# Splits of pre-added weight blocks pinned behind the operation in front of them, and norm steps set further apart, in an attention, experts and squared-ReLU kernel

## The chip, the cores and the metric

The kernel runs on one core of a Trainium2 chip. The metric is the time of one execution on the device in microseconds (us); for each kernel it is measured several times and the median is taken. A profile is one further execution, taken with the hardware profiler: it has a span from the first to the last instruction, and a time of its own.

The core's engines work side by side: TensorE (PE in the profile, its weight loads PEld), VectorE (DVE), ScalarE (ACT), GpSimd (POOL) and SyncE (SP). Each runs its own instructions strictly in the order in which they stand, and an instruction that waits holds up those behind it on the same engine.

## What is computed

Three layers follow each other: windowed attention with a distance bias, a top-1 mixture of eight experts, and a dense layer with a squared ReLU. The change touches the last one alone. Cut to what matters:

```python
def _moe2_ref(x, w_in, w_out):
    h = x @ w_in
    r = np.maximum(h, 0.0)
    g = r * r
    return (g @ w_out).astype(np.float32)

# x: (2304, 512) from the experts, w_in: (512, 2048), w_out: (2048, 512), float32
```

## The kernel before

The last layer (`moe2`, L1366 on) works on the 2304 tokens in nine groups `G` of 256. Every float32 operand is split into two float16 numbers, a high and a low one, and a product is three float16 matmuls (high by high, high by low, low by high). Such a split is two instructions: ScalarE casts to the high half, DVE subtracts it for the low half.

For each group there is a norm (`norm`, L1102), a generator whose steps are run one by one with `next`:

- step 1: ScalarE takes the absolute values (`ab`, L1110), into the buffer `dec`
- step 2: PE sums them (L1115); DVE makes a power of two of the sums (`fac`, L1118 to L1120) and two diagonals `sd` from it (L1124)
- step 3: PE multiplies a matrix of ones by `sd` (L1129), which spreads the factor; DVE scales the group with it (L1130)
- step 4: four subtractions (L1137 to L1140) and the split into `hi` and `lo` (L1150, L1152)

The two halves `m` of the hidden dimension are then handled in turn. `wide1(G, m)` multiplies by `w_in` with seven products of 24 matmuls each (`product`, L1168) in the place of eight (Strassen-Winograd); their results are taken out of PSUM by ScalarE (`keep`, L1188) and DVE (`join`, L1189), squared and split (`square`, L1198; the split is L1195 and L1196). `wide2(G, m)` multiplies by `w_out` for the first three groups, the plain ones (`G < SG`, 3), with 48 matmuls (L1357 to L1359). From group 3 on, `seven` does this step with seven products too, and needs sums and differences of blocks of `w_out`: `T1` to `T4` of eight combined blocks.

The function `mix(k)` makes combined block `k`. Its first part is six additions and subtractions on GpSimd (L1272, L1276 to L1279), in a scratch that is a column of `yT` or `dec`; the first is made to wait for the last DVE instruction of the preceding `wide1` (`end_dve`). Its second part splits the four results: two casts on ScalarE (L1283) and two subtractions on DVE (L1284), queued behind `end_act` and `end_dve`. The table `MIXES` says at which point of the walk over the groups a block is touched: the first time a block is named its first part is issued, the second time its second part. The points are (G, 0) behind `wide2(G, 0)`, (G, 1) inside `wide1(G + 1, 0)` after its second pair of products, (G, 2) behind `wide2(G, 1)` or `seven`, and (G, 3) behind `wide1(G + 1, 1)`.

The norm of group `G + 2` is run inside the work on group `G`. `step` (L1396) issues its next step behind `end_act` and `end_dve`. In plain groups `wide2(G, 0)` calls it four times, once after each 12 matmuls.

Beyond such pins a scheduler orders each engine's queue. `issue_after` orders issue on the same engine and waits for nothing; `behind` is a true wait.

Of the kernel before, what the change touches and what calls it, by code (L numbers as in the profile page):

```python
# [43 lines left out]
RSC = 2.0 ** -9  # L44
# [3 lines left out]
GW = GT * P  # L48
SG = 3
SCRATCH = {0: 0, 1: 1, 2: 1, 3: 2, 4: 3}  # L50
MIXES = {(0, 0): (0,), (0, 1): (0, 1), (0, 2): (1, 2), (0, 3): (2, 3), (1, 0): (3, 4), (1, 2): (4, 5),
         (1, 3): (5,), (2, 0): (6,), (2, 2): (6, 7), (2, 3): (7,)}
STEPS = (((2, 6), ()), ((1, 5), (1,)), ((4,), (1,)), ((1, 5), (1,)), ((1, 5), (1,)), ((3,), (1, 3)), ((3,), (1, 3)),
         ((1, 3, 5, 7), (1, 3)))
SPARE = ((), (), (4, 5, 6, 7), (4, 5, 6, 7), (4, 5, 6, 7), (6, 7), (7,), ())
# [38 lines left out]
class K:  # L94
# [1007 lines left out]
    def norm(self, G, ab, tt):  # L1102


        nc, mp, V = self.nc, self.mp, self.nc.vector
        view = lambda o, n, dt: self.part(o, n, dt) if o is not None else             self.dec.bitcast(dt)[:, :n]
        ab = view(ab, 4 * GW, BF16).rearrange("p (c n) -> p c n", c=4)
        y = self.yT[:, :, G * GW:(G + 1) * GW]
        f = self.fac[G] = mp.tile([P, 2, GT], F32, tag="fac", bufs=4, name="fac")
        nc.scalar.activation(ab, y, AF.Abs)  # L1110
        yield
        l1 = self.bank([P, GT])
        for i in range(GT):
            for c in range(4):
                nc.tensor.matmul(l1[:, i:i + 1], ab[:, c, i * P:(i + 1) * P], self.onesb[:, 0:1],  # L1115
                                 start=c == 0, stop=c == 3)
        m, s = f[:, 0], f[:, 1]
        V.tensor_scalar(m, l1, TINY, HUGE, op0=ALU.max, op1=ALU.min)  # L1118
        V.tensor_single_scalar(m.bitcast(U32), m.bitcast(U32), 0x7F800000, op=ALU.bitwise_and)
        V.reciprocal(s, m)  # L1120
        sds = []
        for i in range(GT):
            sd = mp.tile([P, P], BF16, tag="sd", bufs=2, name="sd")
            V.tensor_scalar(sd, self.idf, s[:, i:i + 1], YSC, op0=ALU.mult, op1=ALU.mult)  # L1124
            sds.append(sd)
        yield
        sb = self.bank([P, GW])
        for i in range(GT):
            nc.tensor.matmul(sb[:, i * P:(i + 1) * P], self.onesb, sds[i], start=True, stop=True)  # L1129
        V.tensor_tensor(y, y, sb.unsqueeze(1).to_broadcast([P, 4, GW]), op=ALU.mult)  # L1130
        yield
        b = y.rearrange("p (h k) (t n) -> p h t k n", h=2, t=2)
        late = G >= SG + 2
        Q = nc.gpsimd if late else V
        t = view(tt, 4 * GW, F32)
        t1, t2, t3, t4 = (t[:, j * GW:(j + 1) * GW].rearrange("p (k n) -> p k n", k=2) for j in range(4))
        Q.tensor_tensor(t1, b[:, 0, 1], b[:, 0, 0], op=ALU.subtract)  # L1137
        Q.tensor_tensor(t2, b[:, 1, 1], t1, op=ALU.subtract)
        Q.tensor_tensor(t3, b[:, 1, 1], b[:, 0, 1], op=ALU.subtract)
        Q.tensor_tensor(t4, b[:, 1, 0], t2, op=ALU.subtract)  # L1140
        if late:
            yield
        hi, lo = self.xts[G] = [self.part(G % 2 * 7168 + 3584 * a, 14 * P, F16).rearrange("p (c n) -> p c n", c=14)
                                for a in range(2)]
        y = y.rearrange("p c (t n) -> p c t n", t=2)
        t = t.rearrange("p (c n) -> p c n", c=8)
        parts = ((0, y[:, :, 0]), (4, y[:, 2:, 1]), (6, t))
        for o, src in parts:
            n = src.shape[1]
            nc.scalar.copy(hi[:, o:o + n], src)  # L1150
            if not late:
                V.tensor_tensor(lo[:, o:o + n], src, hi[:, o:o + n], op=ALU.subtract)  # L1152
        yield
        for o, src in parts if late else ():
            n = src.shape[1]
            V.tensor_tensor(lo[:, o:o + n], src, hi[:, o:o + n], op=ALU.subtract)
        yield
# [22 lines left out]
    def wide1(self, G, m, between=lambda k: None):  # L1180


        nc, V = self.nc, self.nc.vector
        S1, S2, S3, S4, A11, A12, A22 = range(7)
        B11, B21, B22, T1, T2, T3, T4 = range(7)
        c = self.part(14336, 16 * P).rearrange("p (j i t n) -> p j i t n", j=4, i=2, t=2)
        u, p5, z, p1 = (self.part(22528 + 2048 * k, 4 * P).rearrange("p (j n) -> p j n", j=4) for k in range(4))
        keep = lambda dst, ps: nc.scalar.activation(dst, ps, AF.Copy, scale=RSC)  # L1188
        join = lambda dst, ps, x: V.scalar_tensor_tensor(dst, ps, RSC, x, op0=ALU.mult, op1=ALU.add)  # L1189
        mul = lambda *a: self.product(G, m, *a)  # L1190
        n = 2 if G < SG else 4
        g = self.gts[G, m] = [self.ring(F16, [P, 2, 8 * P]) for _ in range(n)]

        def halves(hi, lo, src):
            self.end_act = nc.scalar.copy(hi, src)  # L1195
            self.end_dve = V.tensor_tensor(lo, src, hi, op=ALU.subtract)  # L1196

        def square(i):  # L1198
            ci = c[:, :, i].rearrange("p j t n -> p j (t n)")
            if G < SG:  # L1200
                V.scalar_tensor_tensor(ci, ci, 0.0, ci, op0=ALU.max, op1=ALU.mult)  # L1201
                halves(*(t.rearrange("p i (j n) -> p i j n", j=4)[:, i] for t in g), ci)
                return
            nc.scalar.activation(ci, ci, AF.Relu)  # L1204
            nc.scalar.activation(ci, ci, AF.Square, scale=0.5)
            both = lambda t: (t[:, a].rearrange("p (o j n) -> p o j n", o=2, j=4) for a in range(2))
            if i == 0:
                V.tensor_tensor(p1, c[:, :, 0, 0], c[:, :, 0, 1], op=ALU.subtract)
                halves(*(t[:, 0] for t in both(g[3])), c[:, :, 0, 0])
                halves(*(t[:, 1] for t in both(g[3])), p1)  # L1210
                return
            V.tensor_tensor(p5, c[:, :, 0, 1], c[:, :, 1, 1], op=ALU.add)
            halves(*(g[0][:, a].rearrange("p (j n) -> p j n", j=4) for a in range(2)), ci)
            V.tensor_tensor(u, p5, c[:, :, 0, 0], op=ALU.subtract)
            halves(*both(g[1]), self.part(22528, 8 * P).rearrange("p (o j n) -> p o j n", o=2, j=4))
            V.tensor_tensor(z, c[:, :, 1, 0], u, op=ALU.subtract)
            halves(*(t[:, 0] for t in both(g[2])), z)

        keep(p1, mul(A11, B11))
        keep(u, mul(S2, T2))  # L1220
        V.tensor_tensor(u, u, p1, op=ALU.add)
        keep(p5, mul(S1, T1))
        V.tensor_tensor(z, u, p5, op=ALU.add)  # L1223
        between(0)
        join(c[:, :, 0, 0], mul(A12, B21), p1)
        join(c[:, :, 0, 1], mul(S4, B22), z)
        between(1)
        square(0)
        p7 = mul(S3, T3)
        join(c[:, :, 1, 1], p7, z)  # L1230
        join(u, p7, u)
        join(c[:, :, 1, 0], mul(A22, T4), u)
        square(1)
        between(2)
# [15 lines left out]
    def mix(self, k):  # L1250
# [19 lines left out]
        for o in range(2):  # L1270
            w = self.wo_s[8 * o + k]
            sum_ = Q.tensor_tensor(x[o], *(w[:, a].rearrange("p (o n) -> p o n", o=2) for a in range(2)), op=ALU.add)  # L1272
            if o == 0:
                self.behind(sum_, self.end_dve)
        t1, t3, t4, t2 = (x[o // 2][:, o % 2] for o in range(4))
        Q.tensor_tensor(t1, t3, t1, op=ALU.subtract)  # L1276
        Q.tensor_tensor(t3, t2, t3, op=ALU.subtract)
        Q.tensor_tensor(t2, t2, t1, op=ALU.subtract)
        Q.tensor_tensor(t4, t4, t2, op=ALU.subtract)  # L1279
        yield  # L1280
        with tc.issue_after(self.end_act.ins), tc.issue_after(self.end_dve.ins):
            for o in range(2):
                nc.scalar.copy(y[o][:, :, 0], x[o])  # L1283
                V.tensor_tensor(y[o][:, :, 1], x[o], y[o][:, :, 0], op=ALU.subtract)  # L1284
# [81 lines left out]
    def moe2(self):  # L1366
# [15 lines left out]
        def at(*key):  # L1382
            for n in MIXES.get(key, ()):
                if n in mixing:
                    for _ in mixing.pop(n):
                        pass
                else:
                    mixing[n] = self.mix(n)
                    next(mixing[n])

        mixing = {}
        for G in range(NG):
# [3 lines left out]
            def step():  # L1396
                with tc.issue_after(self.end_act.ins), tc.issue_after(self.end_dve.ins):
                    next(nr)

            if G < SG:  # L1400
                self.wide2(G, 0, lambda k: step())
            else:
                self.seven(G, 0, lambda k: step() if k == 5 else None)
            at(G, 0)
            if more:
                self.wide1(G + 1, 0, lambda k: step() if G >= SG and k < 2 else at(G, 1) if k == 1 else None)
            if G < SG:
                self.wide2(G, 1)
                if G + 1 == SG:
# [67 lines left out]
```

## Time and profile before

| | us |
|---|---|
| timed runs | 768.66, 773.87, 776.87 |
| their median | 773.87 |
| profiled execution, its own time | 769.61 |
| its span | 767.5 |
| PE busy in the span | 715.7 |
| DVE, ACT, POOL busy | 595.9, 444.2, 210.4 |

The span is divided about so: attention and experts until about 410, the plain groups 0 to 2 from there to about 545, then the groups with `seven`. Times in the rows are counted from the start of the span. A row of the timeline gives the start, the duration, engine, line, operation, what it writes and reads, how many instructions are merged in it, and in brackets how long the engine stood idle before it and what released it. A matmul's duration holds the way through the array, so the duration of one matmul is longer than the distance to the next.

### The profile page before, as it was taken

Reading aid. Unit: us, or ns where it says so; the run is one execution under the profiler, and the core shown is the slowest. Engines: PE = TensorE matmul, PEld = TensorE weight load, DVE = VectorE, ACT = ScalarE, POOL = GpSimd, SP = SyncE. Lnnn points to the kernel's source line nnn. Section 1 sums busy time; section 2 is a strip of 40 time slices with the busy share of each in tenths; the row PEclk is TensorE's granted clock in tenths of the full one; section 3 lists DMA queues with packets and bytes.
Section 4 is the critical chain, followed back from the end, with each engine's and each line's share of the span. In section 5 each row is a group of like instructions: output and inputs, shape, how many; then the busy total and the mean of one; then the engine's idle time right before and its main releaser. Section 6 shows DMA issues by size and latency. Waiting matters only on the chain. (4 is left out here: it accounts for less than half of the span.)

```text
span 767.5 us, 19611 instructions
## 1 busy us (share of the span) xinstructions
PE 715.7 (93%) x7979; PEld 603.0 (79%) x7979; DVE 595.9 (78%) x1454; ACT 444.2 (58%) x748; POOL 210.4 (27%) x247
## 2 busy tenths in 40 slices
PE   6989999998879899999898699999999999999996
PEld 5889899787645566788698377676799999999995
DVE  5898888854769988967898776977769696878672
ACT  5878898833456665664643333334657575757561
POOL 4583521434533110000000504733403021211011
PEclk9999999999989999999999989999999999999999
DMA  9895314776689676557614000000000000000000
GB/s 330 293 392 145 79 55 100 242 198 158 204 299 316 217 261 211 188 178 233 207 58 139 2 5 25 2 29 1 29 2 29 2 29 2 29 2 29 2 29 28
DMA packets 35656, 91.71 MB, mean 119 GB/s; under 512 B 5209, under 2 KB 13547, under 8 KB 35547
## 3 DMA queue, kind: packets, MB, share of 16 engines
q1 hardware_dynamic: 29803, 75.77, 30.5%
q0 software_dynamic: 5760, 14.65, 5.8%
q8 instruction: 64, 1.05, 0.6%
q14 instruction: 29, 0.24, 0.1%
HBM read 77.54 MB, written 13.04 MB: 118 GB/s over the span
## 5 line engine op out<-in xcount | busy, mean ns | idle before, releaser
L1176 PEld LDWEIGHTS <-wi 128*128 128x128 f16 x3024 | 172.7, 98 | 11.0 <-issue 9.3
L1309 PEld LDWEIGHTS <-wr 128*128 128x128 f16 x1008 | 98.1, 98 | 12.3 <-issue 1.0
L1195 ACT CAST wr<-work 128x1024 f16<-128x1024 f32 (+1 forms) x72 | 59.9, 832 | 59.2 <-DVE work L1201 42.4
L1176 PE MATMUL ps_a<-work,wi 128*128 128x128 f16 x1344 | 84.9, 220 | 0.0
L850 PE MATMUL ps_c<-work,wr 128*128 128x352 f16 (+5 forms) x256 | 75.1, 297 | 9.2 <-DVE work L799 8.2
L1176 PE MATMUL ps_b<-work,wi 128*128 128x128 f16 x1272 | 80.0, 220 | 1.4 <-DVEq L1064 1.4
L849 PE MATMUL ps_c<-work,wr 128*128 128x352 f16 (+5 forms) x256 | 75.0, 296 | 5.1 <-ACT yT L852 4.2
L851 PE MATMUL ps_c<-work,wr 128*128 128x352 f16 (+5 forms) x256 | 74.9, 296 | 0.0
L1196 DVE TENSOR_TENSOR wr<-work,wr 128x1024 f16<-128x1024 f32 (+1 forms) x72 | 68.9, 980 | 4.4 <-ACT wr L1195 4.4
L310 PE MATMUL ps_a<-yT,wr 128*128 128x192 f32 (+2 forms) x288 | 64.8, 346 | 6.4 <-DMA wr<-in_q_dram 4.7
L322 ACT ACTIVATE pb<-pb,nm 128x192 f32<-128x192 f32 (+2 forms) x144 | 56.3, 433 | 12.4 <-DVE nm L315 11.6
L1337 POOL DMA_INDIRECT out_dram<-o,oid x18 | 25.4, 1412 | 122.1 <-ACT o L1335 87.5
L770 DVE SCALAR_TENSOR_TENSOR wr<-rw,wr 128x1024 f16<-128x1024 f32 x40 | 48.7, 1219 | 8.9 <-ACT wr L769 8.7
L769 ACT ACTIVATE wr<-rw 128x1024 f16<-128x1024 f32 x40 | 42.1, 1058 | 23.1 <-DMA rw<-in_w_dram 22.2
L315 DVE CUSTOM_DVE_ANT_0 pb<-ps_a,bias 128x192 f32<-128x192 f32 (+2 forms) x144 | 44.1, 325 | 10.1 <-PE ps_a L310 9.4
L310 PEld LDWEIGHTS ps_a<-yT,wr 128*128 128x128 f32 x288 | 45.6, 201 | 7.7 <-DMA yT<-in_k_dram 6.4
L1272 POOL TENSOR_TENSOR yT<-wr 128x512 f32<-128x512 f16 x8 | 11.4, 1430 | 144.6 <-ACTq L1064 120.0
L1204 ACT ACTIVATE work<-work 128x1024 f32<-128x1024 f32 x24 | 25.4, 1058 | 38.3 <-DVE work L1189 38.3
L333 PE MATMUL ps_b<-cst,pb 128*128 128x128 f32 x256 | 44.0, 283 | 0.5 <-ACT pts L337 0.4
L851 PEld LDWEIGHTS <-wr 128*128 128x128 f16 x288 | 29.3, 102 | 19.1 <-issue 11.5
L850 PEld LDWEIGHTS <-wr 128*128 128x128 f16 x288 | 29.4, 102 | 14.5 <-issue 7.1
L778 POOL DMA_INDIRECT xg<-xd,idx x21 | 26.6, 1265 | 49.6 <-PE ps_d L786 42.4
(294 smaller groups left out, 1884.6 us busy)
## 6 DMA issues: line engine op xcount, KB each, us to landing
rw<-in_w_dram SPq DMA_DIRECT2D x40, 512.0 KB, 5.9
wi<-in_w_dram SPq DMA_DIRECT2D x20, 512.0 KB, 6.1
rw<-in_wo_dram SPq DMA_DIRECT2D x16, 512.0 KB, 4.2
rw<-in_wi_dram SPq DMA_DIRECT2D x32, 256.0 KB, 4.9
wr<-in_q_dram SPq DMA_DIRECT2D x14, 512.0 KB, 8.0
xd<-xhl POOLq DMA_DIRECT2D x16, 256.0 KB, 6.2
yT<-in_k_dram SPq DMA_DIRECT2D x7, 576.0 KB, 9.3
rw<-in_v_dram SPq DMA_DIRECT2D x12, 325.0 KB, 5.5
```

The costliest lines, as they stand in the source:

```text
L310: nc.tensor.matmul(ps[:, s, first:hi], q[g, u, hh // 4][:, hh % 4, s if u < 4 else 0, :], self.kt[g, hh // 2][:, hh % 2, key0:key0 + hi - ...
L315: self.last_ttr = nc.vector.tensor_tensor_reduce(out=pb[:, s, first:hi], in0=ps[:, s, first:hi], in1=self.bias[:, hh, first - lo:192], sca ...
L322: self.last_exp = nc.scalar.activation(pb[:, s, first:hi], pb[:, s, first:hi], AF.Exp, bias=nm[:, s:s + 1], scale=-1.0)
L333: nc.tensor.transpose(pt[:, t, :, s, :], pb[:, s, t * P:(t + 1) * P], self.idf)
L770: self.nc.vector.scalar_tensor_tensor(t[:, 1], st, sc, t[:, 0], op0=ALU.mult, op1=ALU.subtract)
L849: nc.tensor.matmul(py, wh, hh, start=fc == 0, stop=False)
L850: nc.tensor.matmul(py, wh, hl, start=False, stop=False)
L851: self.last_mm = nc.tensor.matmul(py, wl, hh, start=False, stop=fc == 7)
L1176: self.nc.tensor.matmul(ps[:, j], w[:, kp, a, w0 * P:(w0 + 1) * P], v[:, 2 * x + kp], start=kp + b == 0, stop=kp == 1 and b == 2)
L1195: self.end_act = nc.scalar.copy(hi, src)
L1196: self.end_dve = V.tensor_tensor(lo, src, hi, op=ALU.subtract)
L1309: nc.tensor.matmul(ps[n], x[:, v, j], y[j][:, w], start=m + i + j == 0, stop=m == 1 and i == 2 and j == 3)
```

## The change

Four things are edited. First, every operation that takes results out in `wide1` or ends a norm step (`keep`, `join`, `halves`, and the casts and subtractions at the end of `norm`) is remembered as `fin_act` or `fin_dve`, and `mix` queues its splits and its first addition behind these instead of `end_act` and `end_dve`. Second, block 4 is begun at (1, 1) and block 6 at (2, 1), inside `wide1`, not at (1, 0) and (2, 0). Third, in plain groups the call after the second 12 matmuls of `wide2(G, 0)` issues no norm step any more. Fourth, the step left over is issued in the next `wide1`, after its first three products.

```diff
@@ -48,8 +48,8 @@
-MIXES = {(0, 0): (0,), (0, 1): (0, 1), (0, 2): (1, 2), (0, 3): (2, 3), (1, 0): (3, 4), (1, 2): (4, 5),
-         (1, 3): (5,), (2, 0): (6,), (2, 2): (6, 7), (2, 3): (7,)}
+MIXES = {(0, 0): (0,), (0, 1): (0, 1), (0, 2): (1, 2), (0, 3): (2, 3), (1, 0): (3,), (1, 1): (4,), (1, 2): (4, 5),
+         (1, 3): (5,), (2, 1): (6,), (2, 2): (6, 7), (2, 3): (7,)}
@@ -1147,9 +1147,9 @@
         for o, src in parts:
             n = src.shape[1]
-            nc.scalar.copy(hi[:, o:o + n], src)
+            self.fin_act = nc.scalar.copy(hi[:, o:o + n], src)
             if not late:
-                V.tensor_tensor(lo[:, o:o + n], src, hi[:, o:o + n], op=ALU.subtract)
+                self.fin_dve = V.tensor_tensor(lo[:, o:o + n], src, hi[:, o:o + n], op=ALU.subtract)
@@ -1185,15 +1185,19 @@
-        keep = lambda dst, ps: nc.scalar.activation(dst, ps, AF.Copy, scale=RSC)
-        join = lambda dst, ps, x: V.scalar_tensor_tensor(dst, ps, RSC, x, op0=ALU.mult, op1=ALU.add)
...
+        def keep(dst, ps):
+            self.fin_act = nc.scalar.activation(dst, ps, AF.Copy, scale=RSC)
+
+        def join(dst, ps, x):
+            self.fin_dve = V.scalar_tensor_tensor(dst, ps, RSC, x, op0=ALU.mult, op1=ALU.add)
+
         def halves(hi, lo, src):
-            self.end_act = nc.scalar.copy(hi, src)
-            self.end_dve = V.tensor_tensor(lo, src, hi, op=ALU.subtract)
+            self.end_act = self.fin_act = nc.scalar.copy(hi, src)
+            self.end_dve = self.fin_dve = V.tensor_tensor(lo, src, hi, op=ALU.subtract)
@@ -1271,14 +1275,14 @@
             if o == 0:
-                self.behind(sum_, self.end_dve)
+                self.behind(sum_, self.fin_dve)
...
-        with tc.issue_after(self.end_act.ins), tc.issue_after(self.end_dve.ins):
+        with tc.issue_after(self.fin_act.ins), tc.issue_after(self.fin_dve.ins):
             for o in range(2):
                 nc.scalar.copy(y[o][:, :, 0], x[o])
                 V.tensor_tensor(y[o][:, :, 1], x[o], y[o][:, :, 0], op=ALU.subtract)
@@ -1398,12 +1402,12 @@
             if G < SG:
-                self.wide2(G, 0, lambda k: step())
+                self.wide2(G, 0, lambda k: step() if k != 1 else None)
...
-                self.wide1(G + 1, 0, lambda k: step() if G >= SG and k < 2 else at(G, 1) if k == 1 else None)
+                self.wide1(G + 1, 0, lambda k: step() if k == 0 or G >= SG and k == 1 else at(G, 1) if k == 1 else None)
```

In the changed file the lines from `join` on stand four to seven further down: the joins are L1196 instead of L1189, the squarings L1205 instead of L1201, the splits of a block L1288 instead of L1284, the matmuls of `wide2` L1361 to L1363 instead of L1357 to L1359.

On DVE, in plain group 0 behind `wide2(0, 0)`, the norm of group 2 and the splits of block 0 (the rows that write `xm`) stood so before:

```order
L1118 TENSOR_SCALAR fac<-ps_c 128x2
L1284 TENSOR_TENSOR xm<-yT,xm 128x2x256
L1119 TENSOR_SCALAR fac<-fac 128x2
L1284 TENSOR_TENSOR xm<-yT,xm 128x2x256
L1120 RECIPROCAL fac<-fac 128x2
L1124 TENSOR_SCALAR sd<-cst,fac 128x128 x2
L1165 SCALAR_TENSOR_TENSOR fac<-fac,og 128x2
```

and stand so in the change:

```order
L1118 TENSOR_SCALAR fac<-ps_c 128x2
L1119 TENSOR_SCALAR fac<-fac 128x2
L1120 RECIPROCAL fac<-fac 128x2
L1124 TENSOR_SCALAR sd<-cst,fac 128x128 x2
L1165 SCALAR_TENSOR_TENSOR fac<-fac,og 128x2
```

The two splits have left the norm's chain. Further on in the same queue of the change, inside `wide1(1, 0)`, they stand here (the joins are L1196, the squaring is L1205):

```order
L1196 SCALAR_TENSOR_TENSOR work<-ps_b,work 128x4x128
L1196 SCALAR_TENSOR_TENSOR work<-ps_c,work 128x4x128
L1288 TENSOR_TENSOR xm<-yT,xm 128x2x256 x2
L1205 SCALAR_TENSOR_TENSOR work<-work 128x4x256
L1196 SCALAR_TENSOR_TENSOR work<-ps_a,work 128x4x128
```

They moved behind the second join and in front of the first squaring. On PE, in the same place, the first matmul on `sd` stood behind 21 of the 24 matmuls of the first product of `wide1(1, 0)`; in the change it stands behind five, here with the last of the five and what follows:

```order
L1176 LDWEIGHTS wi_3339
L1176 MATMUL ps_b<-work,wi_3339 128x128
L1129 LDWEIGHTS onesb
L1129 MATMUL ps_a<-sd,onesb 128x128
L1176 LDWEIGHTS wi_3339
L1176 MATMUL ps_b<-work,wi_3339 128x128
L1176 LDWEIGHTS wi_3340
L1176 MATMUL ps_b<-work,wi_3340 128x128
L1129 LDWEIGHTS onesb
L1129 MATMUL ps_a<-sd,onesb 128x128
```

Two matmuls stand between the two on `sd`, as before. In group 1, PE had the pair on `sd` (into `ps_b`) in the middle of `wide2(1, 0)`, five matmuls behind the sums of L1115:

```order
L1357 LDWEIGHTS wr
L1357 MATMUL ps_d<-wr 128x512
L1129 LDWEIGHTS onesb
L1129 MATMUL ps_b<-sd,onesb 128x128
L1129 LDWEIGHTS onesb
L1129 MATMUL ps_b<-sd,onesb 128x128
L1358 LDWEIGHTS wr
```

and has it in the change at the end of `wide2(1, 0)`, in front of `wide1(2, 0)`:

```order
L1363 LDWEIGHTS wr
L1363 MATMUL ps_d<-wr 128x512
L1129 LDWEIGHTS onesb
L1129 MATMUL ps_b<-sd,onesb 128x128
L1129 LDWEIGHTS onesb
L1129 MATMUL ps_b<-sd,onesb 128x128
L1176 LDWEIGHTS wi_3339
```

The pair now has twelve matmuls between itself and the sums, which come one matmul later than before. Group 2 has the same two moves.

## Rows read from the trace of the kernel before

**Rows 1.** The page: each engine's busy us, share of the span, instructions.

```profile
PE 715.7 (93%) x7979; PEld 603.0 (79%) x7979; DVE 595.9 (78%) x1454; ACT 444.2 (58%) x748; POOL 210.4 (27%) x247
```

**Rows 2.** Waits of PE, 400 to 580 us: total us, times, longest.

```profile
PE ps_a L1129 <- DVE sd L1124: 6.5, 1, 6.5
...
PE ps_b L1129 <- DVE sd L1124: 1.4, 2, 0.9
PE ps_a L1115 <- ACT dec L1110: 0.8, 1, 0.8
PE ps_b L1115 <- ACT dec L1110: 0.7, 1, 0.7
PE ps_d L1309 <- DVE wr L1284: 0.6, 1, 0.6
```

**Rows 3.** Timeline of PE, 434 to 450 us: start, duration, instruction, idle before.

```profile
434.03 1.33 PE L1176 MATMUL ps_b<-work,wi 128*128 128x128 f16 x21
441.91 0.27 PE L1129 MATMUL ps_a<-sd,onesb 128*128 128x128 bf16 x1 [6.54 <-DVE sd L1124]
...
446.94 1.50 PE L1176 MATMUL ps_b<-work,wi 128*128 128x128 f16 x24
448.29 1.50 PE L1176 MATMUL ps_c<-work,wi 128*128 128x128 f16 x24
```

**Rows 4.** Timeline of DVE, 433 to 442 us.

```profile
433.10 1.15 DVE L1166 SCALAR_TENSOR_TENSOR fac<-fac 128x2 f32<-128x2 f32 x2
434.16 0.15 DVE L1118 TENSOR_SCALAR fac<-ps_c 128x2 f32<-128x2 f32 x1
437.32 1.23 DVE L1284 TENSOR_TENSOR xm<-yT,xm 128x512 f16<-128x512 f32 x1 [3.01 <-ACT xm L1283]
438.48 0.68 DVE L1119 TENSOR_SCALAR fac<-fac 128x2 uint32<-128x2 uint32 x1
...
441.30 0.75 DVE L1124 TENSOR_SCALAR sd<-cst,fac 128x128 bf16<-128x128 f32 x2
```

**Rows 5.** Timeline of POOL, 430 to 440 us.

```profile
430.64 3.52 POOL L1272 TENSOR_TENSOR yT<-wr 128x512 f32<-128x512 f16 x2 [17.93 <-DVE wr L1196]
434.11 0.74 POOL L1276 TENSOR_TENSOR yT<-yT 128x256 f32<-128x256 f32 x1
...
437.95 1.18 POOL L1277 TENSOR_TENSOR yT<-yT 128x256 f32<-128x256 f32 x1
```

**Rows 6.** Windows of PE: length, busy (instructions), granted clock, DMA share, GB/s.

```profile
436.00:438.00 2.00, 0.00 (x0) 1.00 0.00 0
438.00:440.00 2.00, 0.00 (x0) 0.87 0.00 0
...
444.00:446.00 2.00, 2.00 (x21) 0.50 0.00 0
446.00:448.00 2.00, 2.00 (x36) 0.92 0.03 8
```

**Rows 7.** Timeline, 519 to 527 us: the same norm chain in group 2.

```profile
522.40 0.16 DVE L1118 TENSOR_SCALAR fac<-ps_b 128x2 f32<-128x2 f32 x1 [1.61 <-PE ps_b L1115]
...
523.00 0.48 DVE L1124 TENSOR_SCALAR sd<-cst,fac 128x128 bf16<-128x128 f32 x2
...
523.34 0.41 PE L1129 MATMUL ps_c<-sd,onesb 128*128 128x128 bf16 x2
```

**Rows 8.** Chain that ended last, 400 to 600 us: one matmul of `wide2`.

```profile
452.47 0.22 PE ps_d L1357
```

**Rows 9.** Timelines: DVE after group 0; POOL and ACT on block 6.

```profile
464.09 1.29 DVE L1284 TENSOR_TENSOR xm<-yT,xm 128x512 f16<-128x512 f32 x2 [5.17 <-ACT xm L1283]
...
529.70 3.04 POOL L1272 TENSOR_TENSOR dec<-rw 128x512 f32<-128x512 f16 x2 [18.62 <-PE ps_c L1176]
...
535.13 0.73 POOL L1279 TENSOR_TENSOR dec<-dec 128x256 f32<-128x256 f32 x1
...
545.84 1.12 ACT L1283 CAST yT<-dec 128x512 f16<-128x512 f32 x2
```

## The prediction

> **What bounds the kernel now.** I read the page first: TensorE (PE) is busy for 93% of the span and no other engine comes near [rows 1], so a change counts only where PE stands still or runs slowly. Next I read the waits of PE in the stretch that the change touches, the plain groups of the last layer and the first combined one. The reader should see one wait that towers over the rest: 6.5 us for `sd`, the little diagonal that a norm step hands to PE; the others are under 1 us each [rows 2]. Then I read that place on PE: a product of `wide1` starts at 434.03, 21 of its 24 matmuls issue, and the next instruction, the matmul on `sd`, starts only at 441.91 [rows 3]. On DVE the reason stands in the row order: `fac` (L1118) is done at 434.31, and then comes a split of combined block 0 (L1284) that waits 3.01 us for its ScalarE copy; the next step of the norm (L1119) runs at 438.48, and `sd` at 441.30 [rows 4]. The norm step was ready; it queued behind splits whose data GpSimd was still adding and subtracting [rows 5].
>
> The wait costs more than itself. PE's granted clock is 1.00 in 436 to 438, 0.87 in the next 2 us, 0.50 in 444 to 446, that is 1.2 in place of 2.4 GHz, and returns only in 446 to 448 [rows 6]. So the loss is counted from product start to product start. Three products and two `sd` matmuls lie between 434.03 and 446.94: 12.91 us. At full clock a product takes 448.29 - 446.94 = 1.35 us [rows 3]; three make 4.05, and I allow 0.2 for the two `sd` matmuls (the pair shows 0.41 with its drain [rows 7]). The loss is 12.91 - 4.25 = 8.66 us.
>
> **The change part by part.**
>
> Splits behind the last finishing operation (`fin_act`, `fin_dve`). On DVE nothing stands between L1118 and the two `sd` any more; the two splits of block 0 come after the second join of `wide1(1, 0)`. No instruction is added. On PE the `sd` matmul moves up, to after 5 of the 24 matmuls, which are done issuing at 434.03 + 5 x 1.35/24 = 434.31. What is late next is `sd` itself. Where nothing disturbed DVE, L1118 started at 522.40 and the `sd` matmul at 523.34: 0.94 us [rows 7]. From L1118 at 434.16 that gives 435.10, a remaining wait of 0.79 us. That is the lower bound. Here, however, GpSimd works at the same time. In such company L1119 took 0.68 us and ended at 439.16, just when GpSimd's L1277 ended (437.95 + 1.18 = 439.13) [rows 4, 5]. If each of L1119 and the two `sd` waits for one GpSimd instruction of up to 1.18 us, the wait is 0.79 + 3 x 1.18 = 4.3 us, the upper bound. I take one instruction of 0.74 us [rows 5] in the way, the nearest row being the one L1119 that shows it: 0.79 + 0.74 = 1.53 us. A wait of this length ends before the clock showed any fall [rows 6]. This term is 8.66 - 1.53 = 7.1 us gained, between 4.4 and 7.9.
>
> The Trainium skill (SBUF — State Buffer, section "Who interferes with whom") says that VectorE and GpSimd share one pair of ports under an exclusive lock: a VectorE instruction in a two-port mode, or with two SBUF inputs, and a GpSimd one that reads SBUF block each other for a whole instruction. The L1119 that ended with GpSimd's instruction agrees. By that rule L1119 and both `sd` can each be blocked, and this term would be nearer to 4.4 than to 7.9.
>
> Norm steps further apart. The second step now comes at `k` = 2 of `wide2`, the third at 3, the fourth inside the next `wide1`. The order shows how little of that reaches PE: in groups 1 and 2 the L1115 matmuls come one matmul later, and the `sd` matmuls move from five matmuls behind them to the end of `wide2`, twelve behind. L1115 waits 0.8 and 0.7 us for the `Abs` on ScalarE, which itself waits for the tail of the `wide1` before; that tail is not changed. One matmul of 0.22 us [rows 8] is taken off each wait: 0.44. The two waits on `ps_b` for `sd` sum to 1.4 with the longest 0.9 [rows 2]; the shorter, 0.5, is group 1's, and twelve matmuls (2.6 us) cover the 0.94 us chain with one GpSimd instruction in it. So 0.5 goes. Together 0.9 us.
>
> Blocks 4 and 6 later, and the splits of blocks 3, 4 and 6 earlier in their queues. Each keeps its six GpSimd additions, two ScalarE copies and two DVE splits. I cost these at nothing. The two splits of block 0, now in front of a squaring on DVE, take 1.29 us as a pair, and DVE has 5.17 us idle later in the same group [rows 9]; without that cover they would cost at most 1.3. Block 6 starts behind a join rather than behind a norm's last subtraction; before, its GpSimd work started at 529.70 and ended at 535.86, while its ScalarE copies ran at 545.84 [rows 9]: some 10 us of cover, of which I estimate the later start takes 3 to 4. Without cover PE would wait for the full 3 to 4 us in `seven`. The output DMAs on GpSimd's queue change places with these additions; nothing reads their result. No transfer of SP's queue moves. Block 7 may start a little sooner, which could shorten the 0.6 us wait at L1309 [rows 2]; between 0 and 0.6, I take 0, since its split also queues behind the end of `wide1(3, 1)`.
>
> The sum: 7.1 + 0.9 = 8.0 us. The profiled execution took 769.61 us (span 767.5 and 2.1 around it), so 761.6, between 769.61 - 5.3 = 764.3 and 769.61 - 9.4 = 760.2. That execution is 0.6% faster than the median of the three timed runs, 773.87, from which the same gain gives 765.9. I predict 764.0, between the two.
>
> **The rivals.**
>
> The norm's small operations crawl beside GpSimd. All three are blocked, `sd` comes 4.3 us late, at about 438.6, and by then the clock is falling [rows 6], so the slow part stays too: 446.94 - 441.91 = 5.03 us in place of 51/24 x 1.35 + 0.2 = 3.07, that is 1.96. Gain 8.66 - 4.3 - 1.96 + 0.9 = 3.3: 766.3 in terms of the profiled execution, 770.6 from the median. For it: the pair of L1166 just before takes 1.15 us where GpSimd runs its sums [rows 4, 5]. Against it: L1118 in the same place took 0.15. The port lock of the Trainium skill (SBUF — State Buffer), named above, is this rival's rule.
>
> Slower than before: block 6. Its additions start later, beside a busy DVE; if they end so late that its copies, and then all of block 7, slip, PE waits in `seven(3, 0)` microsecond for microsecond, since that place waits already [rows 2]. It decides from a GpSimd end about 6 us later than I expect (10 of cover less 3 to 4), and the kernel is slower only if it is 6 + 8 = 14 us late. At 20 us late PE loses 14 and gains 8: 769.61 + 6 = 775.6. Against it: the slowest pair of sums in the trace takes 3.52 us [rows 5], so six operations cannot easily last 20 us more.
>
> **How the numbers follow.** The forecast has 0.72, the crawl 0.22, the slower one 0.06. The range: low end from the largest gain, about 9.4 off the fastest runs shown (768.66 to 769.61), 759 to 760, with 2 us for runs that spread over 8 us; high end from the smallest, the crawl from the median at 770.6 and a little more. That gives 757.5 to 772.0. A measurement of this kernel can tell about 1% from no change, here 7.7 us, and my 8.0 lies right on that line: of the forecast's 0.72 I put 0.48 beyond 1% and 0.24 within; of the crawl's 0.22, 0.02 and 0.20; of the last, 0.01 within and 0.05 slower. Faster 0.50, same 0.45, slower 0.05.
>
> **What would show it.** Right: PE's wait on `sd` in `ps_a` falls from 6.5 to between 0.8 and 2.3 us, the granted clock stays 1.00 through that place, and three products span about 6 us in place of 12.9; the 0.5 us wait before the `sd` matmuls of group 1 is gone, while the waits for the `Abs` are 0.6 and 0.5. Wrong: a wait on `sd` over 3 us or a clock below 1.00 there (the crawl); new PE waits on L1284's successor, L1288, over 1 us in `seven(3, 0)` (block 6 or 7 late); or a wait on ScalarE's `keep` in `wide1(2, 0)`, where the copies of block 3 now stand in front of it.

## The result, and the profile after

The changed kernel takes 763.29 us (median of 7 runs, 759.99 to 766.01) against 771.19 for the kernel before (7 runs, 768.24 to 776.87): a ratio of 0.9893, with a 95% interval of 0.9854 to 0.9931. Measured once more beside other runs of before (e9 below) it is 0.9880, interval 0.9864 to 0.9896. The prediction, 764.0 and faster, was right. The profiled execution of the change has a span of 761.2 us, 6.3 less than before.

The page, engines row, answers to [rows 1]; every engine has the work that it had, in a shorter span:

```profile
PE 714.5 (94%) x7979; PEld 601.1 (79%) x7979; DVE 595.0 (78%) x1454; ACT 443.0 (58%) x748; POOL 209.3 (28%) x247
```

The waits of PE from 400 to 580 us (total, times, longest), against [rows 2]:

```profile
PE ps_b L1176 <- DVEq L1064: 1.5, 1, 1.5
PE ps_a L1129 <- DVE sd L1124: 1.4, 1, 1.4
PE ps_b L1129 <- DVE sd L1124: 0.9, 1, 0.9
PE ps_b L1115 <- ACT dec L1110: 0.9, 1, 0.9
PE ps_a L1115 <- ACT dec L1110: 0.6, 1, 0.6
PE ps_d L1313 <- DVE wr L1288: 0.6, 1, 0.6
```

The tower of 6.5 us is 1.4 us high. The first row lies ahead of 430 us, where the change has no part. It stood at 1.4 before, in the line that [rows 2] leaves out, so "the others are under 1 us each" in the prediction was not quite so:

```profile
PE ps_b L1176 <- DVEq L1064: 1.4, 1, 1.4
```

The second row is group 0's; the third is one wait where there were two, since group 1's 0.5 is gone, and the one that is left lies ahead of 430 us too. The two `Abs` waits read 0.6 in group 1 (0.8 before) and 0.9 in group 2 (0.7 before, so it rose). `L1313` is the old L1309. The timeline of PE at the place of [rows 3]:

```profile
435.18 0.35 PE L1115 MATMUL ps_c<-onesb,dec 128*128 128x1 bf16 x8
...
436.04 0.44 PE L1176 MATMUL ps_b<-work,wi 128*128 128x128 f16 x5
437.91 0.22 PE L1129 MATMUL ps_a<-sd,onesb 128*128 128x128 bf16 x1 [1.43 <-DVE sd L1124]
437.96 0.27 PE L1176 MATMUL ps_b<-work,wi 128*128 128x128 f16 x2
438.10 0.22 PE L1129 MATMUL ps_a<-sd,onesb 128*128 128x128 bf16 x1
438.15 1.11 PE L1176 MATMUL ps_b<-work,wi 128*128 128x128 f16 x17
...
441.78 1.50 PE L1176 MATMUL ps_b<-work,wi 128*128 128x128 f16 x24
```

Five matmuls, a wait of 1.43, and the product goes on. Three products take 441.78 - 436.04 = 5.74 us where they took 12.91. The granted clock in windows of the same place, against [rows 6], does not fall:

```profile
436.00:438.00 2.00, 0.57 (x8) 1.00 0.00 0
438.00:440.00 2.00, 2.00 (x38) 1.00 0.00 0
```

On DVE the norm's operations follow one another, with GpSimd's sums of block 0 beside them (DVE, then POOL, against [rows 4] and [rows 5]):

```profile
435.11 1.15 DVE L1166 SCALAR_TENSOR_TENSOR fac<-fac 128x2 f32<-128x2 f32 x2
436.18 0.14 DVE L1118 TENSOR_SCALAR fac<-ps_c 128x2 f32<-128x2 f32 x1
436.36 0.63 DVE L1119 TENSOR_SCALAR fac<-fac 128x2 uint32<-128x2 uint32 x1
437.03 0.17 DVE L1120 RECIPROCAL fac<-fac 128x2 f32<-128x2 f32 x1
437.23 0.82 DVE L1124 TENSOR_SCALAR sd<-cst,fac 128x128 bf16<-128x128 f32 x2
```

```profile
433.05 3.12 POOL L1276 TENSOR_TENSOR yT<-wr 128x512 f32<-128x512 f16 x2 [18.36 <-DVE work L1152]
436.25 0.72 POOL L1280 TENSOR_TENSOR yT<-yT 128x256 f32<-128x256 f32 x1
437.05 0.72 POOL L1281 TENSOR_TENSOR yT<-yT 128x256 f32<-128x256 f32 x1
```

The pair of L1166 ends at 436.26, GpSimd's pair of L1276 at 436.17; L1119 ends at 436.99, GpSimd's L1280 at 436.97; the first matmul on `sd` starts at 437.91, just behind the end of GpSimd's L1281 at 437.77. The reader should keep these three long rows in mind: what is left to gain here is in the 1.15, 0.63 and 0.82 us.

**Reading by stretches.** A whole execution of either kernel spreads over some 8 us, so small differences are read from inside the trace: from the first product of one `wide1` to that of the next. Where an edit does not touch it, such a stretch repeats to 0.1 us. "Start" is the first product of `wide1(1, 0)`; stretch 1 leads from there to `wide1(1, 1)`, stretch 2 to `wide1(2, 0)`, stretch 3 to `wide1(3, 0)`, stretch 4 to the first matmul of `seven(3, 0)`.

| kernel | start | 1 | 2 | 3 | 4 | sum |
|---|---|---|---|---|---|---|
| before | 434.03 | 28.64 | 21.79 | 40.85 | 29.12 | 120.40 |
| the change | 436.04 | 21.46 | 20.82 | 40.82 | 29.11 | 112.21 |
| the change again, e9 | 431.71 | 21.45 | 20.81 | 40.78 | 29.12 | 112.16 |
| e1, splits alone | 435.43 | 20.07 | 23.14 | 40.85 | 29.12 | 113.18 |
| e2, steps alone | 435.14 | 29.23 | 20.82 | 42.54 | 29.12 | 121.71 |
| e3, the change with the old table | 433.18 | 21.45 | 20.81 | 40.88 | 29.12 | 112.26 |
| e4, blocks later | 431.24 | 20.07 | 20.05 | 46.36 | 29.12 | 115.60 |
| e5, early `Abs` | 437.85 | 21.45 | 20.05 | 40.47 | 29.12 | 111.09 |
| e6, splits of block 5 earlier | 437.07 | 21.45 | 20.81 | 39.79 | 29.13 | 111.18 |
| e7, blocks apart | 434.63 | 20.07 | 20.05 | 40.47 | 29.12 | 109.71 |
| e8, all of it | 435.77 | 20.07 | 20.05 | 39.79 | 29.12 | 109.03 |
| e8 again, e10 | 434.26 | 20.06 | 20.06 | 39.79 | 29.12 | 109.03 |

From before to the change the sum falls by 8.19 us. The profiled span fell by 6.3 alone, because the part ahead of it, which the change does not touch, was 2.01 us longer in this one execution; what follows `seven(3, 0)` takes 213.07 us before and 212.95 after. The column "start" shows how much that untouched part moves from run to run: from 431.24 to 437.85.

### The profile page after: what moved, and what is told of

It is laid out like the page before. It is cut to its first block, busy times and chain, and to the rows that moved or that the text cites. A ratio compares the mean times of both kernels' runs of the same rounds, so it can differ in the third digit from the quotient of the medians.

```text
span 761.2 us, 19610 instructions
## 1 busy us (share of the span) xinstructions
PE 714.5 (94%) x7979; PEld 601.1 (79%) x7979; DVE 595.0 (78%) x1454; ACT 443.0 (58%) x748; POOL 209.3 (28%) x247
## 5 line engine op out<-in xcount | busy, mean ns | idle before, releaser
L1176 PEld LDWEIGHTS <-wi 128*128 128x128 f16 x3024 | 170.6, 98 | 5.5 <-issue 4.3
L1313 PEld LDWEIGHTS <-wr 128*128 128x128 f16 x1008 | 98.1, 98 | 12.1 <-issue 0.7
L850 PE MATMUL ps_c<-work,wr 128*128 128x352 f16 (+5 forms) x256 | 73.1, 291 | 11.1 <-DVE work L799 9.9
L849 PE MATMUL ps_c<-work,wr 128*128 128x352 f16 (+5 forms) x256 | 73.1, 291 | 3.6 <-ACT yT L852 2.9
L851 PE MATMUL ps_c<-work,wr 128*128 128x352 f16 (+5 forms) x256 | 73.1, 291 | 0.0
L322 ACT ACTIVATE pb<-pb,nm 128x192 f32<-128x192 f32 (+2 forms) x144 | 55.8, 432 | 13.5 <-DVE nm L315 12.9
L1276 POOL TENSOR_TENSOR yT<-wr 128x512 f32<-128x512 f16 x8 | 11.5, 1440 | 152.9 <-ACTq L1064 121.0
L778 POOL DMA_INDIRECT xg<-xd,idx x21 | 24.0, 1143 | 50.7 <-PE ps_d L786 39.7
```

The source lines that it names most:

```text
L322: self.last_exp = nc.scalar.activation(pb[:, s, first:hi], pb[:, s, first:hi], AF.Exp, bias=nm[:, s:s + 1], scale=-1.0)
L849: nc.tensor.matmul(py, wh, hh, start=fc == 0, stop=False)
L850: nc.tensor.matmul(py, wh, hl, start=False, stop=False)
L851: self.last_mm = nc.tensor.matmul(py, wl, hh, start=False, stop=fc == 7)
L1176: self.nc.tensor.matmul(ps[:, j], w[:, kp, a, w0 * P:(w0 + 1) * P], v[:, 2 * x + kp], start=kp + b == 0, stop=kp == 1 and b == 2)
L1313: nc.tensor.matmul(ps[n], x[:, v, j], y[j][:, w], start=m + i + j == 0, stop=m == 1 and i == 2 and j == 3)
```

## The experiments

Two theories stood against the queue theory of the prediction: that the wider spacing of the norm's steps makes the gain, or that the new table, by taking work off GpSimd, does. The first three kernels are the parts of the change by themselves.

**e1: the splits alone.** The pins of the change, with the table and the steps of before:

```diff
-                self.wide2(G, 0, lambda k: step() if k != 1 else None)
+                self.wide2(G, 0, lambda k: step())
...
-                self.wide1(G + 1, 0, lambda k: step() if k == 0 or G >= SG and k == 1 else at(G, 1) if k == 1 else None)
+                self.wide1(G + 1, 0, lambda k: step() if G >= SG and k < 2 else at(G, 1) if k == 1 else None)
```

> Only the first edit of the change, the splits of a block behind the last finishing operation; the table of blocks and the norm's steps are those of before. Queue theory (the 6.5 us wait came from two splits of block 0 standing inside the norm's chain on DVE): in group 0 PE's wait on sd in ps_a is about 1.4 us as in the change, the granted clock stays 1.00 in 436 to 446 us, the stretch from the first product of wide1(1, 0) to that of wide1(1, 1) is about 21.5 us (28.6 before); group 1 keeps its waits of 0.8 on L1115 and 0.5 on sd, so its stretch stays near 21.8; about 7 us faster than before. Rival, the spacing of the norm's steps makes the gain: the wait of 6.5 and the slow clock remain, under 1.5 us faster. Rival, the later start of blocks 4 and 6 makes it: the same, under 1.5 us faster.

Measured: 761.49 us, ratio 0.9909 (0.9876 to 0.9942). Both rivals fall: without the spacing and the table, 7.2 of the 8.2 us are there (120.40 - 113.18, of 120.40 - 112.21). But the split of it is another than I expected. Stretch 1 is 20.07, better than in the change; stretch 2 is 23.14, worse than before. The waits of PE from 430 to 545 us:

```profile
PE ps_a L1115 <- ACT dec L1110: 2.1, 1, 2.1
PE ps_b L1115 <- ACT dec L1110: 0.7, 1, 0.7
PE ps_b L1129 <- DVE sd L1124: 0.5, 1, 0.5
```

Group 0 has no wait for `sd` any more, and group 1 waits 2.1 for the `Abs`. The timelines of PE, DVE and POOL say why for group 0:

```profile
434.57 0.35 PE L1115 MATMUL ps_c<-onesb,dec 128*128 128x1 bf16 x8
...
435.43 0.44 PE L1176 MATMUL ps_b<-work,wi 128*128 128x128 f16 x5
435.90 0.22 PE L1129 MATMUL ps_a<-sd,onesb 128*128 128x128 bf16 x1
```

```profile
434.50 0.23 DVE L1166 SCALAR_TENSOR_TENSOR fac<-fac 128x2 f32<-128x2 f32 x2
434.96 0.16 DVE L1118 TENSOR_SCALAR fac<-ps_c 128x2 f32<-128x2 f32 x1 [0.23 <-PE ps_c L1115]
435.16 0.17 DVE L1119 TENSOR_SCALAR fac<-fac 128x2 uint32<-128x2 uint32 x1
435.36 0.17 DVE L1120 RECIPROCAL fac<-fac 128x2 f32<-128x2 f32 x1
435.56 0.48 DVE L1124 TENSOR_SCALAR sd<-cst,fac 128x128 bf16<-128x128 f32 x2
```

```profile
432.44 2.00 POOL L1276 TENSOR_TENSOR yT<-wr 128x512 f32<-128x512 f16 x1 [18.47 <-DVE work L1152]
442.18 1.54 POOL L1276 TENSOR_TENSOR yT<-wr 128x512 f32<-128x512 f16 x1 [7.73 <-DVE work L1152]
```

Here all four norm steps are issued in front of block 0, so its pinned sum waits for the norm's last subtraction (L1152, until 442.10). GpSimd stands still through the whole chain, and the DVE operations take 0.23, 0.17 and 0.48 us where the change shows 1.15, 0.63 and 0.82. L1120 is 0.17 in both, L1118, which reads PSUM, 0.16 and 0.14. The late block is paid for in group 1: the `Abs` there stands behind the splits of block 2 (the rows at e5), and starts 18.13 us behind the first product of `wide1(1, 1)` (473.63 - 455.50) where the change has 16.79 (474.29 - 457.50).

The edit holds two pins, one on a block's splits and one on its first addition, and they were not run apart. In the change GpSimd adds beside the chain as it did before, and the wait is 1.4; so the fall from 6.5 to 1.4 comes with the splits out of the chain, and what is left of it goes when GpSimd is idle there as well.

**e2: the steps alone.** The kernel before with the two lines of `wide2` and `wide1` as in the change. With the old table block 4 is begun before the last step of group 3's norm has read the column that is the block's scratch, and block 6 before the norm of group 4 has written and read `dec`; by the code, e2 and e3 overwrite values there, with the same instructions. What they show is time alone.

> Only the third and fourth edits, the norm's steps further apart; the splits stay behind end_act and end_dve and the table is that of before. Queue theory: the wait of about 6.5 us and the clock at 0.50 stay in group 0 (stretch 28.6), group 1 loses its 0.5 us wait on sd and 0.2 of its wait on L1115 (stretch 20.8 instead of 21.8); about 1 us faster than before. Rival, the spacing makes the gain: the wait on sd in group 0 falls to 1.5 us or less, 7 to 8 us faster.

Measured: 770.52 us, ratio 0.9995 (0.9962 to 1.0027). The gain of 0.97 in stretch 2 came as expected. It is more than lost again: stretch 1 has its wait of 6.5 and is 0.59 longer, as the clock falls sooner behind the product's start and returns later, and stretch 3 is 1.69 longer with a wait of 2.6 us on L1115. The two waits (the second ends with GpSimd's first sum of block 6 in `dec`, 0.15 us behind the `Abs`; why the `Abs` itself is late there was not tested), and windows of PE in stretch 1 (last columns: granted clock, DMA share, GB/s), to be held against [rows 6]:

```profile
PE ps_a L1129 <- DVE sd L1124: 6.5, 1, 6.5
PE ps_b L1115 <- POOL dec L1272: 2.6, 1, 2.6
```

```profile
438.00:440.00 2.00, 0.00 (x0) 0.61 0.00 0
440.00:442.00 2.00, 0.00 (x0) 0.50 0.00 0
...
446.00:448.00 2.00, 2.00 (x22) 0.50 0.00 0
448.00:450.00 2.00, 2.00 (x33) 0.83 0.03 8
```

By itself, with the old table, the spacing is worth nothing.

**e3: the change with the old table.** The `MIXES` of before in the changed kernel.

> The change with the table of blocks of before. Queue theory, in which I cost the table at nothing: all three stretches as in the change (21.5, 20.8 and 40.8 us) to 0.3 us, waits of PE on sd 1.4 and 0.9, the same time as the change. Rival, the table carries part of the gain, since block 4 begun earlier keeps GpSimd busy beside the norm of group 3: the stretch of group 1 is over 21.3 us or a wait on sd of group 1 returns; 1 us or more slower than the change.

Measured: 762.00 us, ratio 0.9896 (0.9832 to 0.9959); all stretches as in the change, to 0.06 us. The table carries no time. What it does is in the sentence on e2: it keeps blocks 4 and 6 off scratch that the norm, with its last step later, still uses. So it belongs to the change without earning anything, which the prediction did not see.

**e4: blocks 0 to 4 later.** The change with another table:

```diff
-MIXES = {(0, 0): (0,), (0, 1): (0, 1), (0, 2): (1, 2), (0, 3): (2, 3), (1, 0): (3,), (1, 1): (4,), (1, 2): (4, 5),
+MIXES = {(0, 1): (0,), (0, 2): (0, 1), (0, 3): (1, 2), (1, 0): (2, 3), (1, 1): (3, 4), (1, 2): (4, 5),
```

> The change with blocks 0 to 4 begun and split one point later, so that the first five of GpSimd's six operations on a block no longer fall on the norm chain of group 0. Lock theory (each of the norm's small DVE operations that reads SBUF twice or in a fast mode waits for a whole GpSimd operation beside it): L1119 takes about 0.15 us instead of 0.63, the pairs of L1165 and L1166 in front of it about 0.3 us instead of 0.81 and 1.15, and PE's wait on sd in ps_a falls from 1.43 to 0.9 us or less; the stretch from wide1(1, 0) to wide1(1, 1) is 0.5 to 1.5 us shorter than 21.5. Rival, the wait of 1.43 us is the chain's own length (PE to DVE to PE with four small operations): it stays at 1.2 us or more with GpSimd idle. A second rival is a loss: the splits, one point later, come late for seven(3, 0) and PE gains a new wait of over 1 us there.

Measured: 763.94 us, ratio 0.9934 (0.9905 to 0.9963). The lock theory holds in group 0: L1119 0.17, the pair of L1166 0.23 (that of L1165, further in front, still 0.81, beside the one unpinned sum of block 0, 428.25 to 430.26), no wait on `sd`, stretch 1 shorter by 1.39; stretch 2 by 0.77. The loss came in stretch 3, not in `seven(3, 0)` as the second rival had it. The wait of PE from 430 to 545 us, and its windows:

```profile
PE ps_b L1115 <- ACT dec L1110: 4.1, 1, 4.1
```

```profile
510.00:512.00 2.00, 0.00 (x0) 0.64 0.00 0
512.00:514.00 2.00, 1.46 (x12) 0.50 0.00 0
514.00:516.00 2.00, 2.00 (x6) 0.50 0.00 0
516.00:518.00 2.00, 2.00 (x13) 0.66 0.00 0
518.00:520.00 2.00, 2.00 (x39) 1.00 0.00 0
```

PE waits 4.12 us for the `Abs` of group 2, and the clock falls to 0.50. The wait is 3.25 us longer than in the change, the stretch 5.54: the other 2.3 us are the slow clock. Two rows of DVE in `wide1(2, 0)`, where GpSimd now makes the sums of block 3, show one source of the delay (0.42 and 0.69 in the change):

```profile
474.99 1.38 DVE L1137 TENSOR_TENSOR dec<-yT 128x256 f32<-128x256 f32 x1
...
477.16 1.64 DVE L1225 TENSOR_TENSOR work<-work 128x512 f32<-128x512 f32 x1
```

The delay is handed on from queue to queue: in `wide1(2, 1)` the first `keep` starts 5.80 us behind its product (496.90 - 491.10), behind the casts of block 4, where the change has 1.55 (499.61 - 498.06).

**e5: the `Abs` of group 1 early.** The two waits left on L1115 were each put to a test. In e5 the norm of group 3 begins ahead of `wide1(1, 1)`, and `wide2(1, 0)` issues one step less:

```diff
-                self.wide2(G, 0, lambda k: step() if k != 1 else None)
+                self.wide2(G, 0, lambda k: step() if k > 1 or k == 0 and G != 1 else None)
...
+            if G == 0:
+                nrm[3] = self.norm(3, None, None)
+                next(nrm[3])
```

> The change, with the Abs of group 1's norm issued before wide1(1, 1) instead of in wide2(1, 0). Theory on the wait that is left in group 1: the Abs stands on ScalarE and its buffer behind the two splits of block 3 (they end at the tail of wide1(1, 1)), not behind data of its own; so PE's wait of 0.59 on L1115 goes and the stretch from wide1(1, 1) to wide1(2, 0) falls from 20.82 to about 20.2 us, the other stretches stay (21.46, 40.82). Rival: the wait belongs to the tail of wide1(1, 1) itself, or PE waits for something else there; the stretch stays at 20.8. In time either is under what three rounds can tell from the change.

Measured: 761.65 us, ratio 0.9841 (0.9802 to 0.9881). Stretch 2 is 20.05, a little better than expected, and the wait on L1115 in group 1 is gone. So the `Abs` can run much earlier, and what it stood behind is in the rows of the change (DVE, then ACT):

```profile
472.97 1.28 DVE L1288 TENSOR_TENSOR yT<-yT 128x512 f16<-128x512 f32 x2
```

```profile
474.29 1.06 ACT L1110 ACTIVATE dec<-yT 128x1024 bf16<-128x1024 f32 x1 [1.45 <-DVE yT L1288]
```

By the table these are the splits of block 2, touched behind `wide1(1, 1)`, and not of block 3 as I had written; those follow at 480.55. Stretch 3 became 0.35 us shorter too, which I had not expected. The `Abs` of group 2 starts 16.63 us behind the first product of `wide1(2, 1)` there (515.72 - 499.09), as before the change (16.62), where the change has 16.98; why was not followed.

**e6: the splits of block 5 earlier.** They move into `wide1(2, 1)`, to a new point after its second pair of products:

```diff
-         (1, 3): (5,), (2, 1): (6,), (2, 2): (6, 7), (2, 3): (7,)}
+         (1, 4): (5,), (2, 1): (6,), (2, 2): (6, 7), (2, 3): (7,)}
...
-                self.wide1(G + 1, 1, lambda k: step() if G >= SG and k == 0 else None)
+                self.wide1(G + 1, 1, lambda k: step() if G >= SG and k == 0 else at(G, 4) if k == 1 else None)
```

> The change, with the two splits of block 5 inside wide1(2, 1), after its second pair of products, instead of behind its end. Theory: in group 2 the Abs has to wait until these splits have emptied the buffer they share, which is why PE waits 0.87 us on L1115 there; with the splits some 5 us earlier the wait is gone and the stretch from wide1(2, 0) to wide1(3, 0) falls from 40.82 to about 39.95. Rival: the splits (1.29 us on DVE) delay the squares of wide1(2, 1) by as much, PE waits in wide2(2, 0) or the copies of block 5 are not ready, and DVE stalls: the stretch stays or grows by up to 1.5 us.

Measured: 761.71 us, ratio 0.9844 (0.9813 to 0.9875). Stretch 3 is 39.79, 1.03 shorter, and PE reaches the sums without a wait:

```profile
516.22 0.34 PE L1115 MATMUL ps_b<-onesb,dec 128*128 128x1 bf16 x8
```

So the `Abs` of group 2 stood behind the splits of block 5, and these cost nothing where they stand now. That the shared buffer `dec` is the reason is not shown: in group 1 of the change the `Abs` waits 1.45 us for splits that read `yT`, in group 2 1.46 for those that read `dec`.

**e7: the blocks apart.** e5 with a table that leaves GpSimd idle beside the norm chain of group 0 and puts one block less beside `wide1(2, 0)` than e4:

```diff
+MIXES = {(0, 1): (0, 1), (0, 2): (0, 3), (0, 3): (1, 2), (1, 0): (2, 3), (1, 1): (4,), (1, 2): (4, 5),
+         (1, 3): (5,), (2, 1): (6,), (2, 2): (6, 7), (2, 3): (7,)}
```

> The change with the early Abs of e5 and another table: blocks 0 and 1 begun inside wide1(1, 0), block 3 before block 2, and block 4 where the change has it, so that GpSimd is idle beside the norm chains of groups 0 and 1 and has one block less beside wide1(2, 0) than in e4. If e4's loss in group 2 came from GpSimd slowing DVE beside wide1(2, 0): stretches of 20.1 and 20.1 us in groups 0 and 1 and 40.8 in group 2, 2.2 us better than the change in sum. Rival: group 2's loss came from the two pairs of splits in wide1(2, 0) alone, which are still there: the wait on L1115 in group 2 stays over 3 us, the clock falls to 0.50 and the stretch stays near 46.

Measured: 760.47 us, ratio 0.9846 (0.9812 to 0.9879); stretches 20.07, 20.05 and 40.47. The splits of blocks 2 and 3 are still in `wide1(2, 0)` and do no harm, so the rival falls. What is left of e4's difference is above all the sums of block 3, which no longer run beside `wide1(2, 0)`: L1137 and L1225 take 0.42 and 0.68 us there. The early `Abs` and the order of blocks 2 and 3 differ too and were not taken apart. One thing was not as I expected: beside group 1's chain GpSimd is at work on block 2 here, but there twelve matmuls stand between the sums and `sd`, and no wait is seen.

**e8 and e10: all of it.** e7 with the new point of e6.

> The kernel of e7 with the splits of block 5 as in e6. If the parts add up: stretches of about 20.1, 20.1 and 39.95 us, together 109.2 from the first product of wide1(1, 0) to seven(3, 0) (112.2 in the change, 120.4 before), about 11 us and 1.4% faster than before. Rival: the parts get in each other's way on DVE in groups 1 and 2, and it is no better than the change (8.2 us better than before).

Measured: 760.38 us, ratio 0.9838 (0.9809 to 0.9867). The parts add up in the stretches: 20.07, 20.05, 39.79. In the time of whole runs e5 to e8 cannot be told apart. The two waits on L1115 and those on `sd` in groups 0 and 1 are all gone; from 430 to 575 us PE waits once:

```profile
PE ps_d L1313 <- DVE wr L1288: 0.6, 1, 0.6
```

To see whether the 3.2 us stay to the end, this kernel and the change ran once more beside the same runs of before.

> The change once more, on the same chip and beside the same runs of before as e10. Theory: stretches of 21.5, 20.8 and 40.8 us as in its first profile, whatever the start of wide1(1, 0), which moves by some us from one execution to the next; 1.0 to 1.2% faster than before.

> The kernel of e8 once more. Theory: 20.1, 20.1 and 39.8 us as in e8, 3.2 us (0.4%) faster than the change, 1.4 to 1.6% faster than before. Rival: the 3.2 us are lost behind the plain groups, and it is no faster than the change.

Measured: the change 762.40 us, ratio 0.9880 (0.9864 to 0.9896); e10 758.29 us, ratio 0.9812 (0.9789 to 0.9834). The two intervals do not meet; e10 is 4.1 us under the change, of which the stretches explain 3.1 (112.16 - 109.03). It is the fastest of the kernels tried here.

## Why the prediction was right, step by step

- **The loss of 8.66 us in group 0.** e1, in which the whole wait is gone, has stretch 1 at 20.07 in place of 28.64: 8.57. Right, the slow clock included: the wait was 6.54, so 2.0 us were clock, where I had 8.66 - 6.54 = 2.12.
- **The rest wait of 1.53 us** was 1.43, and the term of 7.1 came as 28.64 - 21.46 = 7.18. That the size fits is in part luck. I had made it of 0.79 us of chain and one GpSimd instruction of 0.74 in the way. But with GpSimd idle (e1) nothing of the wait is left: the chain by itself is covered by PE's own work, and all of the 1.43 is GpSimd's company. My 0.79 took L1118's start in before as undisturbed, where the pair of L1166 in front of it had been slowed to 1.15 us already: in e1 L1118 starts 0.39 us after the sums (434.57 to 434.96), in the change 1.00 (435.18 to 436.18). From L1118 to the `sd` matmul it is 435.90 - 434.96 = 0.94 in e1 and 437.91 - 436.18 = 1.73 in the change, 0.79 more (L1119 0.46 and the pair on `sd` 0.34). So the wait is three holds, at L1166 (1.00 - 0.39 = 0.61), L1119 and `sd`, 1.40 us together; each ends with a GpSimd instruction (436.26 and 436.17; 436.99 and 436.97; the `sd` matmul at 437.91 and 437.77). The Trainium skill (SBUF — State Buffer, section "Who interferes with whom") says that the engine which comes second to the shared ports is blocked until the first one's instruction is over. These ends agree. L1119 took 0.17 with GpSimd idle (e1, e4, e7) and 0.63 beside it, while L1118, which reads PSUM, was as fast in either company. What the rival of the crawl took, three holds of a whole 1.18 us on top of the 0.79, did not come: of the two on `sd` only the first was held (0.63 us, the second 0.27), and the three holds cost 0.34 to 0.61 us each.
- **0.9 us from the norm steps.** In sum it came: 0.97 in stretch 2 and 0.03 to 0.07 in stretch 3 where I had 0.72 and 0.22. The wait for the `Abs` in group 2 rose to 0.9 where 0.5 was forecast: the `Abs` itself came later, 515.04 - 498.06 = 16.98 us behind the first product of `wide1(2, 1)` where before it was 520.82 - 504.20 = 16.62; how it came to be so was not followed. My reading that the `Abs` waits for the tail of the `wide1` before it was wrong: it stood behind the splits of a block, block 2 in group 1 (e5) and block 5 in group 2 (e6), and once these are out of its way both waits are gone.
- **The parts as a sum.** This step failed although its result held: I gave 7.1 to the splits and 0.9 to the steps as if each had it by itself. Alone, the splits give 120.40 - 113.18 = 7.22, with 8.57 gained in group 0 and 1.35 lost in group 1; the steps alone lose 1.31. Together they give 8.19. The steps let block 0 begin sooner (its sums need not wait for the norm's last step), which cuts the wait for the `Abs` in group 1 from the 2.1 us of e1 to 0.6 and costs group 0 the three holds, 1.39 us. The table, which I costed at nothing, is worth nothing in time (e3), but the steps need it.
- **Block 6** started 6.1 us behind the first product of `wide1(3, 0)` (525.23 - 519.14), and its GpSimd work ended at 532.07, 12.9 us behind it, where before it was 10.6 (535.86 - 525.31): 2.4 later, where I took 3 to 4. Its ScalarE copies ran at 536.81, so 4.7 us of cover are left, stretch 4 did not move, and the rival on the slower side did not come about.
- **No sign of being wrong** showed: the wait on L1288 is 0.6 us, the clock stays at 1.00, and PE has no wait on `keep` in `wide1(2, 0)`.
- **The absolute time.** 764.0 lay between 761.6 and 765.9, so with a gain of 8.0 the base was taken as 772; the seven runs of before have 771.19, and 7.9 us were gained. That the base came so near is luck, with runs that spread over 8 us. Against the profiled execution the span fell by less than 8.2 only through the noise ahead of the stretch.

## What to carry to other kernels

A wait that stands on one engine and is caused by the row order of another is found by reading the second engine's timeline for what was ready and had to queue; its price is the wait plus what the clock loses behind it, if it is long enough for the clock to fall. An edit that moves one chain out of another's way also moves when its own data begins, so try the parts alone and read each from anchor to anchor inside the trace: here a stretch repeats to 0.1 us while the whole run moves by several. And small operations on a critical chain should not run beside a stream of additions on GpSimd: leaving GpSimd idle for a few microseconds gained 1.4 us in group 0.

## What the runs showed of the hardware that was not expected

- The slow clock cost about the same behind waits of very different length: 2.0 us behind 6.54 us (before, 28.64 - 20.07 - 6.54) and 2.3 behind 4.12 (e4), but nothing behind 2.15 (e1, group 1, granted clock 1.00 throughout), nor behind 2.59 (e2, group 2, 1.00).
- The company of GpSimd weighs on big DVE instructions too: in `wide1(2, 0)` of e4 one of 128x256 took 1.38 us in place of 0.42 and one of 128x512 1.64 in place of 0.69. Moving GpSimd's work away from one chain can move this cost to another: it stands at the start of the 5.5 us that e4 loses in group 2, which are not lost where these rows are short again (e7).
